# Output stage by d_ff chunks, PSUM banks by estimated end of use, attention tiles read behind a unit's sum: a cosformer attention and SwiGLU kernel

## The chip, the cores and the metric

One core of one Trainium2 chip. The metric is the device time of a run, in microseconds (us): the kernel before has a median of 316.65 us over 5 runs, from 316.18 to 317.08. TensorE (PE) multiplies into PSUM, which has eight banks of 128 partitions x 512 fp32. VectorE (DVE), ScalarE (ACT) and GpSimd (POOL) do the rest, and SyncE (SP), ACT and POOL issue DMAs, each in its own program order.

## The reference

```python
def phi(x, c, s):                       # q and k of shape (8, 8, 576, 64)
    r = np.maximum(x, 0.0)
    return np.concatenate([r * c, r * s], axis=-1)   # c, s: cos and sin of pi/2 * pos/576
kv  = einsum('bhsf,bhsd->bhfd', phi(k), v);  z = phi(k).sum(axis=2)
num = einsum('bhsf,bhfd->bhsd', phi(q), kv)
den = einsum('bhsf,bhf->bhs', phi(q), z)[..., None] + 1e-6
x = (num / den).transpose(0, 2, 1, 3).reshape(4608, 512)
out = (silu(x @ w_gate) * (x @ w_val)) @ w_out       # d_model 512, d_ff 1536, output fp32
```

## The kernel before

**Rows.** The 4608 tokens go in nine rows (`tg` 0 to 8) of 512 tokens, four tiles of 128 tokens each. A row has a hidden stage of twelve slots and an output stage of four. While a row computes, the next rows are prepared: `plan` maps a slot number (16 per row) to functions, `at` enters them, and `slot` calls them when the row's code comes to that slot. So the program order on every engine is written out by hand (`manual_schedule`).

**Hidden stage, rows 0 to 6** (`ffn_fc`): for each of the twelve chunks of d_ff, four matmuls of 512 columns for the gate and four for the value (`ffn_mm`, L564), silu on ACT (L570), the product of both on DVE into `ht` (L575). Two PSUM banks per chunk.

**Hidden stage, rows 7 and 8** (`GATE`, `ffn_by_quarters`): the gate product is a seven-product (Strassen-like) form, in three units `u` of four chunks. A unit has products of 4 matmuls x 256 columns (L621) into banks `a`, `b`, `c`, `e`; between them stand the four value products `V` (L633). ACT copies `a` into `b` (L649) and `e` into `m7` (L653); DVE adds `c = m7 + b` (L659) and `m7 += b` (L668); ACT takes silu (L627), DVE multiplies into `ht` (`mul`, L638). The sums of x that the form needs are L605, those of the weights L597.

**Output stage, rows 2 to 8** (`out_by_quarters`): the same seven-product form over halves of the tokens, of d_ff and of d_model. Order of the products, of 12 matmuls x 256 columns each (`product`, L786): `a`, `e = S3 T3`, `b += S2 T2`, `a +=`, `b += S1 T1`, `c += .. T4`, `b += S4 ..`. In `product` the token half `i` is the outer loop and the d_ff chunk `kc` the inner one. `S1` to `S4` are sums of pieces of `ht` (`token_sum`, L760), made by DVE as the chunks come. ACT copies `a` into `b` (L808) and evicts `e`, `a`, `c` (L811, L799); DVE does L816 (b into c), L827 (b into C22, after S1 T1) and L801 (the last eviction of b). In the last row `b` has a bank for each token half, and L801 and its stores go by halves.

**Preparation.** Per batch `b` of 576 tokens: POOL waits for the turned q of the batch before (`load_behind`, a copy at L998) and loads q, k, v (L131); `phi_q` takes the relu of q on ACT (L266) and multiplies by the cos/sin table on DVE (L283), a quarter at a time; `qturn_dma` turns the result by two DMA transposes on SP (L306); `relu_k` (ACT, L266) and `vmul` (DVE, L287) prepare k and v; `kv_mm` (L333) makes kv, `kv_out2` (L356) copies it out. Per token tile: `a_tile2` multiplies (L448, 8 matmuls, two banks), `x_of` normalises on DVE (L458, L467, L471), `x_turn` turns x by a DMA transpose on SP (L548). Its readers are the next row's matmuls.

**Stores.** `store` (L711) issues two DMAs of 64 partitions x 512 fp32 per tile, on SP; so SP's queue holds, in program order, the transposes of q and x and the stores of each row. The last row's stores are split between SP and ACT (`store_two`, L718).

**Banks.** `take` picks PSUM banks when the program is built: the free ones that were taken or given back longest ago (`touch`, counter `now`). From row 7 on (`loose`) a single bank is picked so that pairs are kept whole where possible. `a_tile2` takes two banks without holding them.

Of the kernel before, what the change touches and what calls it, by code (L numbers as in the profile page):

```python
# [18 lines left out]
def kernel(  # L19
# [32 lines left out]
    GATE = (7, 8)  # L52

# [23 lines left out]
    loose = [False]  # L77

    def take(n, hold=None, fills=False, seeded=False):

        taken = {x for r in held.values() for x in r}
        if loose[0]:
            free = [b for b in range(8) if b not in taken]
            if n == 1:
                bs = [min((b for b in free if filled[b] or not seeded), key=lambda b: (
                    not any(x != b and x + 1 != b and x + 1 in free for x in free), used[b]))]
            else:
                b0 = min((b for b in free if b + 1 in free), key=lambda b: max(used[b:b + 2]))
                bs = [b0, b0 + 1]
            if hold is not None:  # L90
                held[hold] = bs
            for b in bs:
                filled[b] = fills or seeded
            touch(bs)
            return banks[:, bs[0]] if n == 1 else banks[:, bs[0]:bs[0] + 2]
        free = [b for b in range(0, 8, n) if not any(b <= x < b + n for x in taken)
                and (filled[b] or not seeded)]

        b0 = min(free, key=lambda b: (n == 1 and hold is not None and hold[0] == "o" and b ^ 1 not in taken,
                                      sorted(used[b:b + n], reverse=True)))  # L100
        if hold is not None:
            held[hold] = range(b0, b0 + n)
        filled[b0:b0 + n] = [fills or seeded] * n
        touch(range(b0, b0 + n))
        return banks[:, b0] if n == 1 else banks[:, b0:b0 + n]

    def touch(r):
        now[0] += 1
        for x in r:
            used[x] = now[0]  # L110

    def give_back(hold):
        touch(held.pop(hold))
# [171 lines left out]

    def vmul(b, g):
        nc.vector.tensor_tensor(  # L287
            out=v2s[b == 1][:, g, :, :, 0:D],
            in0=(first if b == 0 and g == 0 else {"v": raw_of(b, "v")})["v"][:, g].unsqueeze(2).to_broadcast([P, NC, 2, D]),
            in1=tab, op=ALU.mult,  # L290
        )
# [56 lines left out]

    kv2s = [consts.tile([P, 2, J, 2, D1], BF16, name=f"kv2_{j}") for j in range(2)]

    def kv_out2(b):

        ps = st[b, "kvps"][:, :, 0:4 * J * D1 // 2].rearrange("p e (j w x) -> p e j w x", j=J, w=2)
        for w, eng in enumerate((nc.scalar.copy, nc.vector.tensor_copy)):
            for i in range(2):
                eng(out=kv2s[b % 2][w * D:(w + 1) * D, :, :, i], in_=ps[i * D:(i + 1) * D, :, :, w])  # L356

    def kv_free(b):
        give_back(("kv", b))
# [77 lines left out]
    def a_tile2(t):  # L437

        (b0, c0), (b1, c1) = (divmod(2 * t + r, NC) for r in range(2))
        ps = take(2)  # L440
# [12 lines left out]
        x_of(t, ps)  # L453
# [153 lines left out]
    def ffn_by_quarters(tg, slot_of):  # L607
# [7 lines left out]
        def free(nm):  # L615
            give_back(("g", tg, nm))

        def product(to, u, a, x, first):
            for i in range(2):
                for c in range(KH):  # L620
                    nc.tensor.matmul(out=to[:, i], lhsT=a[:, c, 2 * u + i], rhs=x[:, :, c],  # L621
                                     start=first and i == 0 and c == 0, stop=c == KH - 1, skip_group_check=True)
# [6 lines left out]
        def V(u, i, w):  # L629
            fc = 4 * u + 2 * i + w  # L630
            val[u, i, w] = take(1, ("v", tg, fc), fills=True)
            for kc in range(KC):
# [3 lines left out]
        def mul(u, i, w):  # L636
            fc = 4 * u + 2 * i + w
            nc.vector.tensor_tensor(out=ht[:, fc], in0=gates[u, w][:, i], in1=val.pop((u, i, w)), op=ALU.mult)  # L638
            give_back(("v", tg, fc))
# [5 lines left out]
        for u in range(3):  # L645
# [8 lines left out]
            free("e")  # L654
# [4 lines left out]
            nc.vector.tensor_tensor(out=c, in0=m7, in1=b, op=ALU.add)  # L659
            product(a, u, A12, B21, False)  # L660
            silu(u, 1, 0, a)
            free("a")
            if u:
                mul(u - 1, 1, 1)
# [3 lines left out]
            nc.vector.tensor_tensor(out=m7, in0=m7, in1=b, op=ALU.add)  # L668
            silu(u, 0, 1, m7)
            product(c, u, A22, X4, False)  # L670
            silu(u, 0, 0, c)
            free("c")
            V(u, 1, 0) if u else V(u, 0, 1)
            done()
            if u == 2:
                for n in (1, 2):
                    token_sum(n, 0, 4)
# [6 lines left out]
            free("b")  # L684
            if u:
                V(u, 0, 1)
            mul(u, 0, 1)
            if u:
                done()
                token_sum(*((3, 0, 4) if u == 1 else (4, 0, 4)))  # L690
# [31 lines left out]
    def ffn_out(t, f0=0, f1=None):  # L722
# [16 lines left out]
        store(t)  # L739
# [27 lines left out]
    def out_by_quarters(tg, slot_of):  # L767

        last = tg == NTG - 1
        t0 = tg * OUT  # L770
# [12 lines left out]
        def product(to, a, b, first):  # L783
            for i in range(2):
                for kc in range(HC):
# [31 lines left out]
        token_sum(4, 4, 6)  # L817
# [17 lines left out]
        else:  # L835
            for t in (t0 + 2, t0 + 3):
                store(t)
# [4 lines left out]
        for t in (t0, t0 + 1):  # L842
            store(t, *((slice(HD, d_model), (nc.sync, nc.scalar)) if last else ()))
# [152 lines left out]
    def load_behind(b):  # L996

        nc.gpsimd.tensor_copy(out=hold2, in_=phit[b - 1][0:1, :, 0, 0, 0])  # L998
        load(b, "q")
        if b > 3:  # L1000
            load_kv(b)

# [10 lines left out]
    for n in range(4):  # L1013
        at(SLOTS * (1 + n * (GATE[0] - 1) // 4) + FC + 3, lambda n=n: gate_weight_sum(n))
# [3 lines left out]
    for b in range(2, B):  # L1018
        s0 = SLOTS * (b - 1)
        keng = "dve" if b == 2 else "act"  # L1020
        steps = [lambda b=b, g=g: phi_q(b, g) for g in range(G)]
        steps += [lambda b=b, g=g: (relu_k(b, g, g + 1, keng), vmul(b, g)) for g in range(G)]
        if b == 2:
            fs, tq = [s0 + i for i in (0, 0, 1, 1, 4, 5, 5, 6)], (s0 + 2, s0 + 2)
        else:
            p0 = s0 - SLOTS
            fs, tq = [p0 + 12, p0 + 12] + [p0 + 11 + i for i in range(2, 8)], (p0 + 15, p0 + 16)
            if b == 3:
                fs, tq = [p0 + 12 + i for i in range(4)] + [s0 + 4, s0 + 4, s0 + 5, s0 + 5], (s0 + 2, s0 + 2)
            at(p0 + 3 if b < 5 else p0 + 1, lambda b=b: load_behind(b))  # L1030
        tk = (s0 + 4, s0 + {2: 8, 3: 7}.get(b, 5))
        for s, f in zip(fs, steps):
            at(s, f)
        for e in range(2):
            at(tq[e], lambda b=b, e=e: qturn_dma(b, e))
        at(tk[-1], lambda b=b: kv_mm(b), lambda b=b: kv_out2(b))
        at(tk[-1] + 1, lambda b=b: kv_free(b))
    for t in range(2 * OUT, NTG * OUT):
        tg, i = divmod(t, OUT)
        s = SLOTS * (tg - 1) + (5 if tg > 2 else 4) + 2 * i  # L1040
        if t == 2 * OUT:
            at(s, a_(t, 0))
            at(s + 1, a_(t, 1), turn(t))
        elif tg == 2:
            at((9, 10, 11)[i - 1] + SLOTS, lambda t=t: a_tile2(t), turn(t))
            if i == 2:
                at(11 + SLOTS, load_3)
        else:
            if t in (13, 14, 15):
                s = SLOTS * 2 + t - 4  # L1050
            elif tg - 1 in GATE:
                s = SLOTS * (tg - 1) + ((1, 2, 7, 9) if tg < 6 else (1, 2, 4, 7) if tg < 8 else (1, 2, 5, 6))[i]
            at(s, lambda t=t: a_tile2(t), turn(t))
    for tg in range(1, NTG):
        s0 = SLOTS * tg
        if tg in GATE:
            loose[0] = True
# [9 lines left out]
        for i in range(OUT):  # L1067
            ffn_out(tg * OUT + i)
# [33 lines left out]
```

## Time and profile before

| what | value |
|---|---|
| median of 5 runs | 316.65 us (316.18 to 317.08) |
| the profiled execution: its own time | 316.65 us |
| the profiled execution: span of the trace | 314.9 us |
| busy in the span: PE, DVE, ACT, POOL | 97%, 73%, 46%, 11% |
| granted TensorE clock | 1.00 |
| read from HBM, written | 37.75 MB, 9.44 MB |
| row 3 / 4 / 5 / 6 / 7 / 8 starts at (us of the span) | 120.3 / 152.7 / 185.7 / 218.1 / 250.5 / 281.4 |
| last matmul starts | 310.1 |

The span is counted from the first instruction to the last; 1.75 us of the execution's time lie outside it. The share of busy time is an average; the row starts are the first matmul of each row in the timeline of PE. A matmul record is longer than the distance to the next one, since matmuls are pipelined; so lost time is read from the distances between the starts of groups of matmuls, not from durations.

### The profile page before, as it was taken

To read this page: it belongs to the slowest core of one execution; us is meant where nothing else is said; L and a number is where in the kernel's file an instruction comes from. 1 tells how busy PE (TensorE), PEld (TensorE's weight loads), DVE (VectorE), ACT (ScalarE), POOL (GpSimd) and SP (SyncE) were. 2 spreads that over 40 slices of the span, in tenths; PEclk is the share of its full clock that TensorE was granted. 3 is DMA by queue.
4 is the path that set the end of the run, shared out by engine and by line. 5 is a ranking of instruction groups with operands and counts; after the bars stand their busy time and mean duration, and the time that the engine had idled before them with its cause. 6 is when DMAs were issued, how large, how long until landed. Compare 5 with 4: busy or idle time off the path is not lost.

```text
span 314.9 us, 6775 instructions
## 1 busy us (share of the span) xinstructions
PE 306.5 (97%) x2696; PEld 189.5 (60%) x2696; DVE 228.4 (73%) x458; ACT 143.7 (46%) x264; POOL 35.7 (11%) x62
## 2 busy tenths in 40 slices
PE   8899999999999999999999999999999999999994
PEld 3597455445444585548654764567456866687673
DVE  7874777697678888587748786787779478945772
ACT  8454555763335346334543454336533344324530
POOL 7854102000200200030003000300000000000000
PEclk9999999999999999999999999999999999999999
DMA  7999999996797995999495979598951160014004
GB/s 259 223 198 197 206 205 137 226 135 104 136 209 114 148 147 121 146 118 190 96 152 71 199 152 153 72 192 130 163 90 35 37 149 17 20 35 100 0 2 133
DMA packets 74767, 41.07 MB, mean 130 GB/s; under 512 B 49904, under 2 KB 69872, under 8 KB 74736
## 3 DMA queue, kind: packets, MB, share of 16 engines
q1 hardware_dynamic: 51952, 22.55, 39.1%
q0 software_dynamic: 22192, 17.57, 37.2%
q10 hardware_dynamic: 592, 0.52, 0.5%
q8 instruction: 21, 0.34, 0.5%
q14 instruction: 10, 0.08, 0.1%
HBM read 37.75 MB, written 9.44 MB: 150 GB/s over the span
## 4 chain that ended last, share of the span: by engine, by line
PE 87%; DVE 7%; DMA 2%; ACT 2%; issue 1%; DVEq 0%; ACTq 0%
PE banks L564 45%; PE banks L786 17%; PE banks L729 6%; PE banks L633 5%; PE banks L621 5%; PE banks L333 3%; PE banks L448 2%; DMA xT<-x 2%; DVE ht L638 1%; DVE sums L760 1%; DVE x L471 1%; PE banks L494 1%; PE banks L430 1%; DVE v L287 1%; DVE ht L575 1%
## 5 line engine op out<-in xcount | busy, mean ns | idle before, releaser
L564 PE MATMUL banks<-xT,wg_sb 128*128 128x512 f16 (+2 forms) x368 | 86.6, 360 | 0.2 <-DMA xT<-x 0.2
L564 PE MATMUL banks<-xT,wv_sb 128*128 128x512 f16 (+2 forms) x368 | 86.6, 360 | 0.0
L570 ACT ACTIVATE sg<-banks 128x512 bf16<-128x512 f32 (+2 forms) x92 | 51.5, 560 | 76.3 <-PE banks L564 73.7
L575 DVE TENSOR_TENSOR ht<-sg,banks 128x512 f16<-128x512 bf16 (+2 forms) x92 | 58.0, 637 | 29.9 <-PE banks L564 22.8
L564 PEld LDWEIGHTS <-wv_sb 128*128 128x128 f16 x368 | 35.5, 98 | 37.4
L564 PEld LDWEIGHTS <-wg_sb 128*128 128x128 f16 x368 | 33.9, 98 | 31.8 <-issue 0.5
L786 PEld LDWEIGHTS <-ht 128*128 128x128 f16 x336 | 32.5, 98 | 4.2
L786 PEld LDWEIGHTS <-sums 128*128 128x128 f16 x252 | 24.4, 98 | 4.2 <-issue 0.8
L633 PE MATMUL banks<-xT,wv_sb 128*128 128x512 f16 x96 | 24.3, 379 | 0.0
L283 DVE TENSOR_TENSOR r_q<-raw_q,tab 128x1152 bf16<-128x1152 bf16 x24 | 17.6, 754 | 7.4 <-ACT raw_q L266 7.1
L729 PE MATMUL banks<-wo_sb,ht 128*128 128x512 f16 x96 | 22.7, 379 | 0.0
L471 DVE TENSOR_TENSOR x<-banks,rec 128x512 f16<-128x512 f32 (+1 forms) x32 | 21.6, 674 | 1.3 <-PE banks L430 0.3
L786 PE MATMUL banks<-wo_sb,ht 128*128 128x256 f16 x168 | 20.6, 273 | 0.0
L287 DVE TENSOR_TENSOR v<-raw_v,tab 128x1152 bf16<-128x1152 bf16 x27 | 19.9, 751 | 0.3 <-ACT raw_v L849 0.3
L786 PE MATMUL banks<-wt_sb,sums 128*128 128x256 f16 x168 | 19.8, 273 | 0.1
L786 PE MATMUL banks<-wt_sb,ht 128*128 128x256 f16 x168 | 19.5, 272 | 0.0
L799 ACT ACTIVATE ob<-banks 128x512 f32<-128x512 f32 x14 | 8.4, 597 | 21.8 <-PE banks L786 21.8
L638 DVE TENSOR_TENSOR ht<-sg,banks 128x512 f16<-128x512 bf16 x24 | 15.5, 681 | 2.4 <-ACT sg L627 2.4
L266 ACT ACTIVATE raw_k<-raw_k 128x576 bf16<-128x576 bf16 (+1 forms) x25 | 17.0, 694 | 0.0
L760 DVE TENSOR_TENSOR sums<-ht 128x1024 f16<-128x1024 f16 (+1 forms) x28 | 15.5, 553 | 0.4
L998 POOL COPY hold<-phit 1x2 bf16<-1x2 bf16 x5 | 0.9, 177 | 128.5 <-DMA phit<-r_q 128.5
L266 ACT ACTIVATE raw_q<-raw_q 128x576 bf16<-128x576 bf16 x24 | 15.4, 675 | 0.0
(121 smaller groups left out, 333.8 us busy)
## 6 DMA issues: line engine op xcount, KB each, us to landing
out_dram<-ob SPq DMA_DIRECT2D x67, 128.0 KB, 2.4
raw_k<-in_k_dram POOLq DMA_DIRECT2D x7, 576.0 KB, 9.1
raw_q<-in_q_dram POOLq DMA_DIRECT2D x6, 576.0 KB, 6.5
raw_v<-in_v_dram POOLq DMA_DIRECT2D x6, 576.0 KB, 11.7
wo_sb<-in_moe_w_out_dram POOLq DMA_DIRECT2D x3, 512.0 KB, 12.8
wg_sb<-in_moe_w_gate_dram POOLq DMA_DIRECT2D x5, 256.0 KB, 9.1
wv_sb<-in_moe_w_val_dram POOLq DMA_DIRECT2D x5, 256.0 KB, 9.5
wo_sb<-in_v_dram SPq DMA_DIRECT2D x2, 576.0 KB, 4.3
```

The source lines that it names most:

```text
L266: nc.scalar.activation(out=out, in_=in_, func=AF.Relu)
L283: nc.vector.tensor_tensor(out=st[b, "q"][:, g], in0=o.unsqueeze(2).to_broadcast([P, NC, 2, D]), in1=tab, op=ALU.mult)
L287: nc.vector.tensor_tensor(out=v2s[b == 1][:, g, :, :, 0:D], in0=(first if b == 0 and g == 0 else {"v": raw_of(b, "v")})["v"][:, g].unsquee ...
L471: nc.vector.tensor_tensor(out=st["x", t].rearrange("p (y e d) -> p e y d", e=2, d=D)[:, :, ys], in0=ps[:, :, 0:2 * J * D1].rearrange("p e ...
L564: nc.tensor.matmul(out=st["f", tg, fc, lo][i], lhsT=(wg_sb, wv_sb)[i][:, kc, fs], rhs=xT[tg][:, ts, kc], start=(kc == 0), stop=(kc == KC - 1))
L570: nc.scalar.activation(out=sg[:, 0:n], in_=st["f", tg, fc, lo][0], func=AF.Silu, scale=DOWN)
L575: nc.vector.tensor_tensor(out=ht[:, fc, r:r + n], in0=st.pop(("s", tg, fc, lo))[:, 0:n], in1=ps[1], op=ALU.mult)
L633: nc.tensor.matmul(out=val[u, i, w], lhsT=wv_sb[:, kc, fc * P:(fc + 1) * P], rhs=xT[tg][:, :, kc], start=(kc == 0), stop=(kc == KC - 1))
L638: nc.vector.tensor_tensor(out=ht[:, fc], in0=gates[u, w][:, i], in1=val.pop((u, i, w)), op=ALU.mult)
L729: nc.tensor.matmul(out=o_ps[t], lhsT=ht[:, fc, r:r + P], rhs=wo_sb[:, fc], start=(fc == 0), stop=(fc == FC - 1))
L760: nc.vector.tensor_tensor(out=o[:, lo:hi], in0=x[:, lo:hi], in1=y[:, lo:hi], op=op)
L786: nc.tensor.matmul(out=to[i][:, 0] if len(to) == 2 else to[0][:, i], lhsT=a[:, kc, i * P:(i + 1) * P], rhs=b[:, kc], start=first and kc == ...
```

## The change

- `product` of the output stage has `kc` outermost and the token half `i` innermost.
- Stores of rows 1 to 7 are issued by POOL instead of SP.
- `take` in rows 7 and 8 picks the single free bank whose estimated end of use is earliest. The estimate is in matmul rows (`rows`, moved on by `LATE["M"]`, `["V"]`, `["O"]`, `["X"]`); `give_back` gets a lateness per use. `a_tile2` holds its banks until its x is recorded.
- In rows 7 and 8 an attention tile at certain slots puts its x (L458, L467, L471, L548) and the freeing of its banks into `behind`, which is emptied after `c = m7 + b` and after `m7 += b`. In the same way DVE's half of `kv_out2`. `mul(u - 1, 1, 1)` moves behind `m7 += b`; `S2` of the first chunks moves behind two more `mul`, `S4` of the first chunks into the output stage.
- Slots come from tables: `ROW` per batch (phi of q, turning, k and v, kv), `TILES` per row. Batch 3 and 4 stay; for batches 5 and 6 the phi of q moves from slots 12, 12, 13, 14 to 8, 9, 12, 12 and 6, 8, 9, 12, the turning from 15 and 16 to 13, k and v from 15 to 18 to 13 to 16. Tiles of rows 5 to 7 move from slots 5, 7, 9, 11 to 2, 4, 7, 9; those made in row 7 from 1, 2, 5, 6 to 0, 3, 5, 7.
- Batch 7's phi of q is 18 ACT instructions of 128 x 256 (`phi_q_part`) instead of 4 relus on ACT and 4 multiplies on DVE.
- q of batches 6 and 7 is loaded one row earlier, behind k and v of the batch before.
- The weight sums L597 are at the ends of rows 1, 2, 3, 4 instead of 1, 2, 4, 5.

The order of instructions is the same up to row 2 on PE, DVE and ACT, and the number of matmuls is the same (2696).

```diff
+    AHEAD = 6
+    WSUM = (31, 47, 63, 79)
+    ROW = {2: ((16, 16, 17, 17), 18, (20, 21, 21, 22), 8), 3: ((12, 13, 14, 15), 18, (20, 20, 21, 21), 7),
+           4: ((12, 12, 13, 14), 15, (15, 16, 17, 18), 5), 5: ((8, 9, 12, 12), 13, (13, 14, 15, 16), 5),
+           6: ((6, 8, 9, 12), 13, (13, 14, 15, 16), 5), 7: ([4 + i // 2 for i in range(18)], 13, (12, 13, 14, 15), 3)}
+    TILES = {2: (0, 9, 10, 11), 3: (5, 9, 10, 11), 4: (5, 7, 9, 11), 5: (2, 4, 7, 9), 6: (2, 4, 7, 9), 7: (2, 4, 7, 9), 8: (0, 3, 5, 7)}
+    LATE = dict(M=44, V=87, O=131, X=26, x=150, v=(190, 250, 120, 150), e=130, a=90, c=170, b=110, k=120)
...
-                bs = [min((b for b in free if filled[b] or not seeded), key=lambda b: (
-                    not any(x != b and x + 1 != b and x + 1 in free for x in free), used[b]))]
+                bs = [min((b for b in free if filled[b] or not seeded), key=lambda b: used[b])]
...
-    def touch(r):
+    def touch(r, late=1):
         now[0] += 1
+        if loose[0]:
+            for x in r:
+                used[x] = rows[0] + late
+            return
...
+    def phi_q_part(b, c, w):
+        if (b, "q") not in st:
+            st[b, "q"] = rel.tile([P, G, NC, 2, D], BF16, name="r_q")
+        nc.scalar.activation(out=st[b, "q"][:, :, c, w], in_=raws[b, "q"][:, :, c], func=AF.Relu,
+                             scale=csk[:, c, w:w + 1])
...
-        x_of(t, ps)
+        if later:
+            behind.append(lambda: (x_of(t, ps), give_back(("a2", t), LATE["x"]), x_turn(t)))
+        else:
+            x_of(t, ps)
+            give_back(("a2", t), LATE["x"])
...
             nc.vector.tensor_tensor(out=c, in0=m7, in1=b, op=ALU.add)
+            while behind:
+                behind.pop(0)()
             product(a, u, A12, B21, False)
             silu(u, 1, 0, a)
-            free("a")
-            if u:
-                mul(u - 1, 1, 1)
+            free("a", LATE["a"])
             V(u, 0, 0) if u else V(u, 1, 0)
             done()
             product(b, u, W1, X1, False)
             nc.vector.tensor_tensor(out=m7, in0=m7, in1=b, op=ALU.add)
+            while behind:
+                behind.pop(0)()
             silu(u, 0, 1, m7)
+            if u:
+                mul(u - 1, 1, 1)
...
             if u == 2:
-                for n in (1, 2):
-                    token_sum(n, 0, 4)
+                token_sum(1, 0, 4)
...
             mul(u, 0, 1)
+            if u == 2:
+                token_sum(2, 0, 4)
             if u:
                 done()
-                token_sum(*((3, 0, 4) if u == 1 else (4, 0, 4)))
+            if u == 1:
+                token_sum(3, 0, 4)
...
+        queues = (nc.gpsimd, nc.gpsimd) if tg > 0 else None
...
-            for i in range(2):
-                for kc in range(HC):
+            rows[0] += LATE["O"]
+            for kc in range(HC):
+                for i in range(2):
                     nc.tensor.matmul(out=to[i][:, 0] if len(to) == 2 else to[0][:, i],
...
-        token_sum(4, 4, 6)
+        token_sum(4, 0 if tg in GATE else 4, 6)
...
-                store(t)
+                store(t, queues=queues)
...
-        load(b, "q")
+        if b < AHEAD:
+            load(b, "q")
         if b > 3:
             load_kv(b)
+        if AHEAD <= b + 1 < B:
+            load(b + 1, "q")
```

## The prediction

> **What bounds the kernel now.** First the page's line of busy time.
>
> ```profile
> PE 306.5 (97%) x2696; PEld 189.5 (60%) x2696; DVE 228.4 (73%) x458; ACT 143.7 (46%) x264; POOL 35.7 (11%) x62
> ```
>
> PE has work nearly all the time. Then the busy time by row (stretch, length, PE, PEld, DVE, ACT, POOL, granted clock, DMA share, GB/s); rows 4, 6, 7 and 8:
>
> ```profile
> 152.60:185.70 33.10, 32.83 (x295) 19.59 (x294) 24.63 (x46) 15.34 (x27) 2.41 (x4) 1.00 0.83 138
> 218.20:250.50 32.30, 32.30 (x293) 19.55 (x291) 23.17 (x45) 12.31 (x22) 0.00 (x0) 1.00 0.48 86
> 250.50:281.40 30.90, 30.40 (x251) 22.11 (x249) 22.95 (x45) 12.27 (x22) 0.00 (x0) 1.00 0.24 52
> 281.40:310.40 29.00, 28.97 (x218) 20.93 (x215) 19.17 (x34) 12.19 (x23) 0.00 (x0) 1.00 0.22 52
> ```
>
> The clock is full; DVE has 7 to 10 us to spare in each row, ACT 17 or more. The matmuls stay the same 2696, so only PE's waits, its start and its tail can change. Busy PE hides short waits; I read them from distances between starts in PE's timeline (start, length, line). Without a wait, eight matmuls of 512 columns take 1.727 us (.216 each), twelve of 256 columns 1.30 (.1087 each).
>
> ```profile
> 182.03 1.91 PE L786 MATMUL banks<-wt_sb,ht 128*128 128x256 f16 x16
> 183.97 1.47 PE L786 MATMUL banks<-wo_sb,sums 128*128 128x256 f16 x12
> 185.68 1.02 PE L564 MATMUL banks<-xT,wg_sb 128*128 128x512 f16 x4 [0.24 <-DMA xT<-x]
> ...
> 256.67 0.60 PE L621 MATMUL banks<-xT,wg_sb 128*128 128x256 f16 x4
> 257.61 0.60 PE L621 MATMUL banks<-kvt,wgs_sb 128*128 128x256 f16 x4 [0.35 <-DVE x L471]
> ...
> 266.95 1.03 PE L633 MATMUL banks<-xT,wv_sb 128*128 128x512 f16 x4
> 268.05 0.60 PE L621 MATMUL banks<-kvt,wgs_sb 128*128 128x256 f16 x4
> ...
> 273.26 3.04 PE L786 MATMUL banks<-wt_sb,sums 128*128 128x256 f16 x24
> 276.13 1.04 PE L786 MATMUL banks<-wo_sb,ht 128*128 128x256 f16 x8
> ```
>
> From 182.03, sixteen matmuls need 1.74 and take 1.94: **.20** lost ahead of S4's product. From 183.97 to 185.68 is 1.71 for 1.30: **.41** before row 5, for xT. At 256.67 four need .435 and take .94: **.51** for L471's x, whose read frees the bank. From 266.95 it is 1.10 for .865: **.245**, c and m7 late behind an attention tile, sums and `mul`. From 273.26 it is 2.87 for 2.61: **.25**, for S2's last chunk (L760). In the same way: .20 before S4's product in rows 2, 3, 5 (.17 in row 3), .06 at 265.21, .13 in row 8 at 304.08. Behind 16 us these make 2.4 us in all; the losses before that lie ahead of the first reordered code.
>
> **The change part by part.** Sums are against this execution: its own time is 316.65 us, span 314.9 and 1.75 outside; that is also the median of the runs shown.
>
> *S4's product waits for the bank that L827 empties.* DVE's timeline in row 2 shows why that is late:
>
> ```profile
> 117.55 0.76 DVE L283 TENSOR_TENSOR r_q<-raw_q,tab 128x1152 bf16<-128x1152 bf16 x1
> 118.22 0.68 DVE L827 SCALAR_TENSOR_TENSOR ob<-banks,ob 128x512 f32<-128x512 f32 x1
> ```
>
> Multiplies of phi of q are ahead of L827, three to a row at .67 from start to start. Row 2 keeps them (batch 4's slots stay): nothing. Rows 3 and 4 lose them from the output stage, row 5 altogether: .17 + .20 + .20 = **.56** gained (rounded from .565). What is late next: L827 follows L816 at .65, and PE's 24 matmuls between (2.6) cover both.
>
> *xT before row 5.* The last tile's transpose was issued at 178.60 and landed at 185.54, while loads for batch 6 (issued 170.5 to 172) ran until 185.16. Now q of batch 6 is loaded a row earlier, and row 5's tiles are made at slots 2, 4, 7, 9 instead of to 11, some 3.5 us earlier (a slot is 1.73): **.41** gained.
>
> *Row 7's gates.* The e product gets another bank (the earliest free by the estimate), tiles come at slots 2, 4, 7, 9 behind c and m7, so c is no longer behind a tile's 1.05 us of DVE; S2's first chunks come later, two `mul` earlier. I put DVE's new order against PE's starts: e's bank is read .5 before it is wanted, c and m7 come .15 to .5 early. What the change puts behind them, x and its transpose on SP, is wanted a row later; its banks by PE's next tile, over three slots on. .51 + .06 + .245 = **.82**.
>
> *Chunks outermost in `product`.* S2's last sum was .25 late in row 7 and .13 in row 8. The last two chunks' first use moves from 4 matmuls (.43) into a product to 8 (.87): .44 more, over both. **.25 + .13 = .38** gained. Chunk order costs PE nothing that I see: the same weights and shapes.
>
> Gains: .56 + .41 + .82 + .38 = **2.17**.
>
> *The tail pays.* In the last row the two halves of b end apart now:
>
> ```profile
> 309.75 0.42 DVE L801 TENSOR_SCALAR ob<-banks 128x256 f32<-128x256 f32 x1 [1.54 <-PE banks L786]
> 310.39 1.50 ACTq L711 DMA_DIRECT2D out_dram<-ob  x2
> 310.41 0.42 DVE L801 TENSOR_SCALAR ob<-banks 128x256 f32<-128x256 f32 x1 [0.23 <-PE banks L786]
> ```
>
> Half 0 is complete six matmuls (.65) before half 1; with halves innermost, one (.11). Its L801 and store start .55 later; half 1's L801 stands behind it, .3 later. The first of ACT's two stores takes .75 of its 1.50, so the end moves by .1 to .55. I take **.5**, since ACT's pair is the last issue to end.
>
> *Stores to POOL.* In rows 1 to 7, 56 issues of .75 (L131's row on POOL) leave SP for POOL, whose 11% leave room. SP had eight of them in its way:
>
> ```profile
> 119.59 5.68 SPq L711 DMA_DIRECT2D out_dram<-ob  x8
> 125.37 7.70 SPq L306 DMA_TRANSPOSE phit<-r_q  x2
> ...
> 135.79 0.18 POOL L998 COPY hold<-phit 1x2 bf16<-1x2 bf16 x1 [30.55 <-DMA phit<-r_q]
> 136.24 0.75 POOL L131 DMA_DIRECT2D raw_q<-in_q_dram  x1 [0.28 <-PE banks L448]
> ```
>
> The transposes can start when r_q ends (120.92). From 125.37 to the second landing, 135.64, it took 10.27: so 121.0 + 10.27 = 131.3. A store waits on POOL for its eviction now, and behind it stand only the copy and the loads. POOL ends its eight stores at 119.7 + 8 x .75 = 125.7, so they are hidden; POOL's copy and loads go 4.4 earlier. Before, q of batch 5 landed at 142.62; in after it lands at about 138.3. It is now wanted at slot 8 of row 3, by its relu at about 137.9, and PE stands still only from 139.3 on. So it costs nothing, with 1.0 us to spare. The extra load (q of batch 6) adds 3.5 to 4 to the three loads' 13.6; the last tile's xT of row 3 then lands by 151.5, wanted at 152.6: nothing.
>
> POOL stores have a rule against them. "SBUF — State Buffer" of the Trainium skill, section "SBUF: two separate sides", says that issuing a DMA from GpSimd is held up while DVE runs an operation in a mode that takes both ports. At 170.5 to 172.7 POOL's three issues took .75, .75, .76 beside DVE's L575 and L760, and those took .68 to .69 as elsewhere: no hold-up is seen here. By the rule at its worst each store would wait for one DVE operation, 8 x (.75 + .69) = 11.5, ending at 131.2 instead of 125.7, still not behind the transposes' landing: no change of the sum by either.
>
> *Batch 7's phi of q on ACT* (18 pieces, table as scale). Row 5's DVE loses 4 x .75 = 3.0; ACT gets 18 operations instead of four at .675 (L266). None of this form stands in the trace. The nearest rows are L504, with a scale from a table on 128x260, at .476, and L266 itself, 576 wide, at .69; below L356's .375 nothing suggests. At .48 ACT has .56 (silu) + 2 x .48 = 1.52 in a slot of 1.73: hidden. At .69 it has 1.94, .21 too much in each of nine slots (less in the last, 8 count): 1.7 late, against .7 that the second pair of banks gives; **1.0** lost. I take .48, the like form; so nothing.
>
> *The weight sums* (3 x .95 in a row) move from the end of row 5 to that of row 3, behind its L801: DVE has 8 us to spare there: nothing; up to .2 if L575 of the next row's first slot comes late.
>
> Sum: 316.65 - 2.17 + .5 = **315.0 us**, span about 313.2. Own range 314.2 (tail .1, and .4 that short distances hid from me) to 315.8 (tail .55, a third of the gains given back).
>
> **Rivals.**
>
> - *ACT becomes the bound in row 5.* For it: two extra operations beside each silu; against: L504's .476. Price 1.0 from above: 316.0.
> - *It doesn't do what it says.* The planner's estimates put a bank or a tile no better than before: row 7 loses .8 elsewhere, rows 4 and 5 (.6) get other waits for xT. Left: 2.17 - 1.4 - .1 (S4 in one row) - .5 = .2: 316.5. For it: c and m7 have only .15 of slack. Against: the order by hand shows no such wait.
> - *Slower: q of batch 5 comes late in row 3.* Phi of q at slot 8 needs it at 137.9; before it landed at 142.62. If the transposes don't move up (SP held by something else, or the stores' packets delay them), it lands at 142.6, ACT's relu stands there with silu behind it, and both pairs of banks fill: PE loses 142.6 - 139.3 = 3.3. 316.65 + 3.3 - 1.65 = 318.3. It decides from a landing at 141.0 on (1.65 eaten). For it: four loads now share the queues, and stores come beside them; against: the 4.4 us by which the copy on POOL moves up.
>
> **How the numbers follow.** The forecast has .58, ACT as the bound .16, not as it says .10, late q .16. About 0.2% (.63 us) is what a measurement of this kernel can tell from no change. Faster: .58 and half of ACT's case, which ends at that edge: .66. Same: the other half and the third case: .18. Slower: .16. The range reaches from 314.2 over the first three cases to 317.0, since about .2 may be left out.
>
> **What the profile after would show.** Right: 2696 matmuls; S4's product late by .2 in row 2 alone; row 5 without idle time for xT; no distance over .1 too long in rows 7 and 8; the transposes of row 3 on SP at 121, POOL's copy at 131.5, q landing near 138; pieces of phi at .48; the end .5 further behind the last matmul. Wrong: L564 or L621 waiting for ACT in row 5 (long pieces), PE still at 139 to 143 (q), or tiles whose x, now behind a sum, hold the banks that the next product wants. Early losses ahead of 16 us should stand as they are.

## The result, and the profile after

The changed kernel takes a median of 318.91 us over 27 runs (316.47 to 323.66), the kernel before 316.72 over 47 (316.17 to 318.00); the ratio is 1.0048, with a 95% interval of 1.0037 to 1.0060. So it is slower by half a per cent, and the prediction (315.0, range 314.2 to 317.0) is wrong. The ratio leaves out executions far above the others; the first profile is of one of these, 322.26 us with a span of 320.5, and a second one, of an execution at 318.80, comes from experiment 13.

The line of busy time of the changed kernel:

```profile
PE 308.3 (96%) x2696; PEld 190.5 (59%) x2696; DVE 225.6 (70%) x452; ACT 148.0 (46%) x278; POOL 65.6 (20%) x118
```

The matmuls are the same 2696. The last starts at 315.62, 5.5 us later than before. By stretch (same columns as in the prediction; the stretches are those of the kernel before), two of them have idle PE, rows 3 and 5:

```profile
120.00:152.60 32.60, 30.18 (x265) 17.66 (x264) 24.20 (x46) 14.70 (x28) 7.43 (x13) 1.00 0.96 158
...
185.70:218.20 32.50, 29.99 (x248) 16.42 (x246) 20.55 (x39) 16.93 (x35) 5.94 (x11) 0.95 0.83 123
```

Row 5 has a clock of .95 as well. All waits that the prediction wanted gone are gone: row 7 goes through without a distance over .1 too long, row 5 doesn't wait for xT, S2's last chunk is in time in rows 7 and 8, S4's product is .2 late in row 2 alone. Where .51 was lost in row 7, the two starts are .43 apart now, as long as four matmuls take:

```profile
257.30 0.60 PE L651 MATMUL banks<-xT,wg_sb 128*128 128x256 f16 x4
257.73 0.60 PE L651 MATMUL banks<-kvt,wgs_sb 128*128 128x256 f16 x4
```

The loss is new. Row 3, in the timelines of PE, ACT, SP and POOL:

```profile
143.56 0.29 PE L473 MATMUL banks<-kv,phit 128*128 128x65 bf16 x4
144.25 0.29 PE L473 MATMUL banks<-kv,phit 128*128 128x65 bf16 x4 [0.40 <-DVE ht L604]
146.56 1.47 PE L825 MATMUL banks<-wo_sb,ht 128*128 128x256 f16 x12 [2.02 <-DVE x L500]
```

```profile
142.12 0.68 ACT L277 ACTIVATE raw_q<-raw_q 128x576 bf16<-128x576 bf16 x1 [4.00 <-DMA raw_q<-in_q_dram]
142.71 0.58 ACT L599 ACTIVATE sg<-banks 128x512 bf16<-128x512 f32 x1
```

```profile
121.60 11.01 SPq L323 DMA_TRANSPOSE phit<-r_q  x2
```

```profile
120.38 4.21 POOL L748 DMA_DIRECT2D out_dram<-ob  x8 [14.13 <-ACT ob L838]
134.38 0.18 POOL L1037 COPY hold<-phit 1x2 bf16<-1x2 bf16 x1 [9.79 <-DMA phit<-r_q]
134.87 0.79 POOL L142 DMA_DIRECT2D raw_q<-in_q_dram  x1 [0.31 <-issue]
```

Read it from the bottom up. POOL's stores go out at 120.4 to 124.6, as forecast; the transposes start at 121.60, as forecast. But now they run beside each other: the two transposes' issue takes 11.01 on SP (7.70 before), the second lands at 134.23 instead of 131.3, POOL's load follows at 134.87, and q of batch 5 lands at 142.10, 7.2 behind its issue (6.4 before). ACT's relu (L277) of slot 8 stands 4.00 us for it, with silu (L599) behind; PE fills its banks and loses .56 + 2.19 = 2.75 us.

Row 5, in the timelines of PE, ACT and SP:

```profile
205.37 0.29 PE L473 MATMUL banks<-kv,phit 128*128 128x65 bf16 x4 [1.43 <-DVE ht L604]
206.74 0.37 PE L473 MATMUL banks<-kv,phit 128*128 128x65 bf16 x4 [1.08 <-ACT sg L599]
206.92 1.90 PE L593 MATMUL banks<-xT,wg_sb 128*128 128x512 f16 x4
208.61 1.81 PE L593 MATMUL banks<-xT,wv_sb 128*128 128x512 f16 x4
```

```profile
196.46 0.60 ACT L599 ACTIVATE sg<-banks 128x512 bf16<-128x512 f32 x1 [1.14 <-PE banks L593]
203.22 0.91 ACT L300 ACTIVATE r_q<-raw_q,cs_all 128x256 bf16<-128x256 bf16 x2 [6.16 <-DMA xT<-x]
```

```profile
185.04 10.64 SPq L323 DMA_TRANSPOSE phit<-r_q  x2
```

ACT's first piece of batch 7's phi (L300) stands 6.16 us. The profile puts xT as the releaser, but this piece reads only q and the table. What ended at 203.07 is the second transpose of batch 6, and it reads `r_q`, which has a single buffer: the piece writes the buffer that the transpose still reads. That transpose took 14.42 us from its issue, beside eight stores, and the pair 18.0 from the first issue. PE loses 1.60 + 1.24 us, and then L593 goes at half speed for eight matmuls (1.90 for four): 1.6 more.

Sum: 310.10 (last matmul before) - 2.17 (the gains, as forecast) + 2.75 + 2.84 + 1.6 + .5 (the first 119 us, in which the matmuls started later in this execution) = 315.6. It closes, so only these two places need a cause.

### The profile page after: what moved, and what is told of

Read it like the earlier page. It is cut to its first block, busy times and chain, and to the rows that moved or that the text cites. A ratio compares the mean times of both kernels' runs of the same rounds, so it can differ in the third digit from the quotient of the medians.

```text
span 320.5 us, 6798 instructions
## 1 busy us (share of the span) xinstructions
PE 308.3 (96%) x2696; PEld 190.5 (59%) x2696; DVE 225.6 (70%) x452; ACT 148.0 (46%) x278; POOL 65.6 (20%) x118
## 4 chain that ended last, share of the span: by engine, by line
PE 82%; DMA 10%; SPq 2%; DVE 2%; ACT 2%; issue 1%; DVEq 0%; POOL 0%; POOLq 0%; ACTq 0%
PE banks L593 38%; PE banks L825 20%; PE banks L766 7%; PE banks L664 6%; PE banks L651 6%; DMA phit<-r_q 3%; DMA ht<-in_k_dram 3%; DMA xT<-x 2%; DMA raw_q<-in_q_dram 2%; PE banks L473 2%; PE banks L350 2%; SPq L323 1%; PE banks L523 1%; SPq L171 1%; PE banks L454 1%
## 5 line engine op out<-in xcount | busy, mean ns | idle before, releaser
L593 PE MATMUL banks<-xT,wg_sb 128*128 128x512 f16 (+2 forms) x368 | 87.6, 363 | 0.0
L593 PE MATMUL banks<-xT,wv_sb 128*128 128x512 f16 (+2 forms) x368 | 87.4, 363 | 0.1
L599 ACT ACTIVATE sg<-banks 128x512 bf16<-128x512 f32 (+2 forms) x92 | 51.3, 559 | 69.8 <-PE banks L593 63.6
L593 PEld LDWEIGHTS <-wv_sb 128*128 128x128 f16 x368 | 35.7, 99 | 38.1 <-issue 1.4
L748 POOL DMA_DIRECT2D out_dram<-ob x56 | 29.4, 534 | 125.8 <-ACT ob L838 121.0
L593 PEld LDWEIGHTS <-wg_sb 128*128 128x128 f16 x368 | 33.7, 98 | 31.0 <-issue 1.0
L294 DVE TENSOR_TENSOR r_q<-raw_q,tab 128x1152 bf16<-128x1152 bf16 x20 | 14.7, 753 | 6.3 <-ACT raw_q L277 6.2
L277 ACT ACTIVATE raw_k<-raw_k 128x576 bf16<-128x576 bf16 (+1 forms) x25 | 16.7, 694 | 0.0
L473 PEld LDWEIGHTS <-phit 128*128 128x128 bf16 (+1 forms) x240 | 10.4, 101 | 10.2 <-issue 4.6
```

The source lines that it names most:

```text
L277: nc.scalar.activation(out=out, in_=in_, func=AF.Relu)
L473: nc.tensor.matmul(out=ps[ms, e, g * D1:(g + 1) * D1], lhsT=phit[b][:, e, g, c:c + n].rearrange("p c s -> p (c s)"), rhs=kv2s[b % 2][:, e, ...
L593: nc.tensor.matmul(out=st["f", tg, fc, lo][i], lhsT=(wg_sb, wv_sb)[i][:, kc, fs], rhs=xT[tg][:, ts, kc], start=(kc == 0), stop=(kc == KC - 1))
L599: nc.scalar.activation(out=sg[:, 0:n], in_=st["f", tg, fc, lo][0], func=AF.Silu, scale=DOWN)
L748: (queues or (nc.sync, nc.sync))[e].dma_start(out=out_v[idx // NC, idx % NC][:, cols], in_=ob_of(t)[e * SH:(e + 1) * SH, cols])
```

## The experiments

Theory 1: slots were moved ahead of what they need; phi of batch 5 stands for q's landing, batch 7's for the buffer `r_q`. Theory 2: stores on POOL now run beside the transposes of q and lengthen them, so that things land later than the prediction had them. Rival 3: the planner's banks, the tiles behind sums, or a full ACT cost time.

**1: batch 5's old slots.**

```diff
-           5: ((8, 9, 12, 12), 13, (13, 14, 15, 16), 5),
+           5: ((12, 12, 13, 14), 15, (15, 16, 17, 18), 5),
```

> The changed kernel, with batch 5's phi of q, turning and k and v put back to the slots they had before (12, 12, 13, 14; 15; 15 to 18); all else as changed. Theory 1 (slots that want data too early): in row 3 the relu of slot 8 stood for q of batch 5, which landed at 142.10, and PE lost 0.56 + 2.19 = 2.75 us between 143.6 and 146.6. With the old slots that wait is gone: 2.7 us less than the changed kernel, no gap above 0.3 us in row 3; the stall of row 5 (2.84 us and a clock of half for 8 matmuls after it) stays. S4's product is .2 late in row 3 again. Theory 2 (stores on POOL run beside the transposes of q, which then take 12.6 to 18.0 us from first issue to last landing instead of 10.3 to 11.9): it gains the same 2.7 here, since the late landing hurts only the early slots; but it says that transposes keep their 12.6 and more. Rival 3 (the planner's banks or the tiles behind sums hold PE): row 3 keeps its gap, no change.

314.90 median (314.69 to 320.21, 12 runs), ratio to the kernel before .9947 (.9930 to .9964): 4.0 below the changed kernel, more than the 2.7 expected, and faster than before. No gap in rows 3 and 5, S4's product .2 late in rows 2 and 3. The last matmul starts at 308.02, 2.08 ahead of the kernel before: the prediction's gains less row 3's .17 are 2.0. q landed at 141.51, as late as ever; nobody stood for it. In row 5 the first piece still stood 3.13 us (transposes 15.1 from first issue to POOL's copy behind them), but PE's banks covered it:

```profile
197.08 0.91 ACT L300 ACTIVATE r_q<-raw_q,cs_all 128x256 bf16<-128x256 bf16 x2 [3.13 <-DMA xT<-x]
```

**2: phi of batch 7 in its own buffer.**

```diff
...
-            st[b, "q"] = rel.tile([P, G, NC, 2, D], BF16, name="r_q")
+            st[b, "q"] = raw_q[:, 1:3].rearrange("p n g c d -> p (n g c d)").rearrange("p (g c w d) -> p g c w d", c=NC, w=2, d=D)
```

(in `phi_q_part`; `raw_q`, a pool of three buffers before, is made one tile of three, of which batch 7 uses the first)

> The changed kernel, with phi of q of batch 7 written to two raw_q buffers that are idle by then instead of the single r_q buffer; same slots, same 18 pieces on ACT. Theory 1: the first piece, at slot 4 of row 5, stood 6.2 us for the transposes of batch 6 that still read r_q (landed 203.07), silu behind it; PE lost 1.60 + 1.24 us, then 1.6 by the halved clock. Without the shared buffer these are gone: 2.8 to 4.4 us less than a run that has them, nothing in row 5 above 0.2; the 2.75 of row 3 stay. The pieces take .45 to .48 each. Theory 2 gives the same here. Rival 3 (ACT is too full in row 5 with 18 pieces of .46, about two per slot): row 5 loses 1.0 or more even without the shared buffer.

318.96 median (317.37 to 321.08, 7 runs), ratio 1.0071 (1.0043 to 1.0099). In the profile, at 317.37, the piece goes without a wait and row 5 is whole, so the buffer was the wait; ACT's pieces take .45 each and don't fill ACT, so that part of rival 3 falls. Row 3 still loses .12 + 2.19 = 2.3. But the other runs are no faster than the changed kernel, so row 5 isn't what makes its usual time.

```profile
196.10 0.89 ACT L300 ACTIVATE raw_q<-raw_q,cs_all 128x256 bf16<-128x256 bf16 x2
```

**3: all stores on SP.**

```diff
-        queues = (nc.gpsimd, nc.gpsimd) if tg > 0 else None
+        queues = None
...
-            ffn_out(tg * OUT + i, queues=(nc.gpsimd, nc.gpsimd))
+            ffn_out(tg * OUT + i)
```

> The changed kernel with all stores on SP again, in the order of the program; the slots as changed. Theory 1 alone (the slots are too early whatever the queues do): row 3 stalls 3.3 (q of batch 5 lands at 142.6 as before), row 5 still stalls about 2.8; time as the changed kernel, within 1 us. Theory 2 (the stores beside the transposes make these late): the transposes of batch 6 are issued ahead of row 4's stores and land 10.3 to 11.9 after their first issue, at 9 us into row 5 instead of 15; row 5 loses under 0.5 and keeps its clock: 3 to 4 us less than a run of the changed kernel that has the stall. Row 3 still loses 3.3, because there the transposes stand behind the eight stores on SP.

322.40 median (320.31 to 324.22, 6 runs), ratio 1.0171 (1.0136 to 1.0207). Theory 2 is right in row 5: the transposes of batch 6, ahead of the stores on SP now, took 9.9 us instead of 18.0, and PE lost nothing there. In row 3 both theories were right in kind and I was short in size: the transposes started at 126.59 behind the stores, q landed at 145.71, and PE lost 6.3 us, then 1.6 by a halved clock. With PE still from 139.3 on, the prediction's price formula gives 145.7 - 139.3 = 6.4.

```profile
145.74 0.68 ACT L277 ACTIVATE raw_q<-raw_q 128x576 bf16<-128x576 bf16 x1 [7.61 <-DMA raw_q<-in_q_dram]
```

**4: 1 and 2 together.**

> Both: batch 5's old slots, and batch 7's phi of q in its own buffer; stores on POOL, banks, tiles, output order as changed. Theories 1 and 2: no stall in rows 3 and 5, clock 1.00; what the prediction counted as gains is left, less the .17 of row 3: 315.2 us, 1.5 below the kernel before, and all runs within 1 us of each other. Rival 3: something else of the change costs as well, 316.5 or more.

315.72 median (315.00 to 320.06, 12 runs), ratio .9968 (.9953 to .9982). The profile, at 315.32, has no stall; but the median is .8 above experiment 1. Between the two profiles, .2 is a later start and .4 lies behind the last matmul (5.3 us to the end of the span; 4.9 in experiment 1). Experiment 2 ends 5.3 behind it too, but so do experiments 3 (5.4) and 7 (5.3), which don't have the tile of three buffers; so the tile isn't shown to be the cause, and the longer end stays open.

**5: slots as changed, q of batch 5 loaded a row earlier.**

```diff
-    AHEAD = 6
+    AHEAD = 5
```

> The changed kernel with its early slots, but q of batch 5 too is loaded a row earlier (AHEAD 5 instead of 6): in row 2, behind q, k and v of batch 4. Theory 1 (the early slots of row 3 stand for q's landing, and for nothing else): the relu at slot 8 finds its q, the gap of 2.2 to 2.8 us in row 3 is gone. In its place a fourth load stands in row 2: it ends about 3.5 later, at 120.6, and with it xT of row 3's last tile, wanted at 120.3: up to 1 us lost there. 316 to 317, with single runs higher where row 5 stalls. Rival (the work of slot 8 and 9 itself is too much for ACT and DVE in row 3): the gap stays though q is there.

315.72 median (315.06 to 316.92, 12 runs), ratio .9968 (.9953 to .9983). The relu of slot 8 runs at once, at 137.66, and row 3 has no gap: it was the landing of q, not the work. xT of the last tile landed at 119.72, in time for row 3. In this profile (316.62) row 5 loses 1.9 behind `r_q`.

```profile
137.17 0.60 ACT L599 ACTIVATE sg<-banks 128x512 bf16<-128x512 f32 x1 [1.39 <-PE banks L593]
137.66 0.68 ACT L277 ACTIVATE raw_q<-raw_q 128x576 bf16<-128x576 bf16 x1
```

**6: the kernel before, with batch 5's early slots alone.**

```diff
+            if b == 5:
+                fs, tq = [p0 + i for i in (8, 9, 12, 12, 13, 14, 15, 16)], (p0 + 13, p0 + 13)
```

> The kernel before with one part of the change: phi of q of batch 5 at slots 8, 9, 12, 12 of row 3, its turning at 13, k and v at 13 to 16. Theory 1: q lands at 142.6 as in the kernel before, PE stands still from 139.3 on, so 3.3 us lost, .2 gained at S4 in row 3 (it is no longer behind multiplies): 319.8; 321.4 where the clock halves after the stall. Rival (the stall needs the stores on POOL): no stall, 316.5.

321.72 median (321.33 to 322.52, 5 runs), ratio 1.0151 (1.0131 to 1.0172), as theory 1 has it for a halved clock. q landed at 142.76; PE lost .78 + .78 + 2.19 = 3.75, and then 25 distances of matmuls were doubled. So this one part makes the loss, without any store on POOL:

```profile
144.01 0.29 PE L448 MATMUL banks<-kv,phit 128*128 128x65 bf16 x4 [0.61 <-ACT sg L570]
144.91 0.29 PE L448 MATMUL banks<-kv,phit 128*128 128x65 bf16 x4 [0.61 <-DVE ht L575]
147.22 1.01 PE L786 MATMUL banks<-wo_sb,ht 128*128 128x256 f16 x4 [2.02 <-DVE x L471]
```

**7: experiment 1 with all stores on SP** (the edits of 1 and 3).

> Experiment 1 (batch 5's old slots) with all stores on SP again. Theory 2 (stores on POOL lengthen the transposes, SP's stores delay their start, and PE waits for neither now): transposes take 10 to 11 us from first issue to landing in row 5 instead of 12 to 15, they start 4 later in row 3; time the same as experiment 1 within .4 (314.7 to 315.3), with fewer single runs above 317. Rival (stores on POOL bring part of the gain): 315.5 or more, with a wait for xT or q in rows 3 to 5.

317.15 median (316.46 to 319.54, 12 runs), ratio 1.0016 (.9997 to 1.0035): 2.25 above experiment 1, so the rival holds. The transposes started at 126.01, four loads followed from 138.88 to a last landing at 155.76, and row 4 stood for its last tile's xT:

```profile
155.08 1.04 PE L593 MATMUL banks<-xT,wg_sb 128*128 128x512 f16 x4 [2.22 <-DMA xT<-x]
```

In row 5 the transposes took 9.9 as in experiment 3. So stores on POOL lengthen the transposes, and yet pay: without them the transposes of row 3 land at 138.28 instead of 134.06 (experiment 1), the four loads end 3.9 later (155.76, 151.86 in experiment 1), and xT is late. Here, and in experiment 3, the pair took 12.3 in row 3, where the kernel before had 10.27 in the same order on SP; why isn't known.

**8: the kernel before, chunks outermost in `product`.**

```diff
-            for i in range(2):
-                for kc in range(HC):
+            for kc in range(HC):
+                for i in range(2):
```

> The kernel before with chunks outermost in the output product, nothing else. By the prediction's steps: the waits of .25 (row 7) and .13 (row 8) for S2's last chunk go, and the end lies .1 to .5 further behind the last matmul: 316.4 to 316.8, no change that can be told. Rival (the order of the products changes something else, such as weight loads that PE waits for): a steady excess in L786's starts, 0.5 us or more over seven rows.

316.42 median (316.06 to 316.82, 12 runs), ratio .9982 (.9972 to .9992). S2's waits in rows 7 and 8 are gone, the other waits stand (that for xT before row 5 is .16 in this profile); the end is 4.9 us behind the last matmul's start instead of 4.8.

**9: experiment 1 with the old choice of single banks.**

```diff
-                bs = [min((b for b in free if filled[b] or not seeded), key=lambda b: used[b])]
+                bs = [min((b for b in free if filled[b] or not seeded), key=lambda b: (
+                    not any(x != b and x + 1 != b and x + 1 in free for x in free), used[b]))]
...
-        if loose[0]:
-            for x in r:
-                used[x] = rows[0] + late
-            return
```

> Experiment 1 (no stall in row 3) with the choice of single banks as in the kernel before: pairs kept whole, order of use by the counter. The prediction's step for row 7: without the estimate, products of row 7 get banks that an attention tile still holds; the e product waits .3 to .6, c's or b's products some tenths: .5 to .9 us more than experiment 1 (315.4 to 315.8). Rival (the new slots and order on DVE alone take these waits away): the same as experiment 1, and nothing over .1 in row 7.

315.06 median (314.79 to 315.86, 5 runs), ratio .9946 (.9926 to .9966): as experiment 1, nothing over .1 in rows 7 and 8. The rival holds: the estimate of the banks' end of use brings nothing that shows. (Row 4 waited .3 for xT in this profile, where the fourth load landed at 152.2; so did experiment 14, .2.)

**10: experiment 1 with the tiles' x at once, not behind a sum.**

```diff
-            later = tg - 1 in GATE and s in (0, 1, 3, 4, 7, 8)
+            later = False
```

> Experiment 1, with the attention tiles of rows 7 and 8 normalised on DVE at once instead of behind c = m7 + b and m7 += b. The prediction's step: c stands behind 1.05 us of a tile's DVE work again; a product of row 7 waits .2 to .3 at two or three places: .3 to .8 more than experiment 1 (315.2 to 315.7). Rival (the tiles' new slots are enough): the same as experiment 1, no gap above .1.

316.35 median (315.69 to 317.92, 12 runs), ratio .9985 (.9967 to 1.0002): 1.4 above experiment 1. Row 7 loses .32, .25, .14 and .26, two of these here (L690 is c = m7 + b); .27 in row 5 is the `r_q` wait.

```profile
253.08 1.03 PE L664 MATMUL banks<-xT,wv_sb 128*128 128x512 f16 x4
254.26 0.60 PE L651 MATMUL banks<-kvt,wgs_sb 128*128 128x256 f16 x4 [0.16 <-DVE banks L690]
...
266.71 1.03 PE L664 MATMUL banks<-xT,wv_sb 128*128 128x512 f16 x4
267.82 0.60 PE L651 MATMUL banks<-kvt,wgs_sb 128*128 128x256 f16 x4
```

**11: the kernel before, stores of rows 1 to 7 on POOL.**

```diff
+        if 4 <= t < 32:
+            queues = (nc.gpsimd, nc.gpsimd)
```

> The kernel before, with the stores of rows 1 to 7 issued by POOL, nothing else. The prediction: costs nothing; transposes of rows 2 to 5 start 4 to 5 us earlier and land 4.4 earlier, q of batch 5 at 138.3. Theory 2: the stores run beside the transposes, which take 12.6 or more instead of 10.3; they start 4.3 earlier and land 1.5 to 2 earlier, q of batch 5 at 141.5; row 5's wait for xT (.41) goes, since the loads end earlier: 316.2 to 316.8.

316.25 median (316.02 to 316.96, 11 runs), ratio .9982 (.9971 to .9993). The transposes went from 121.14 to 134.05, 12.9 us; q landed at 141.80. Row 5's wait for xT is gone, the others stand (S2's in row 7 with .13 instead of .25).

```profile
121.14 11.05 SPq L306 DMA_TRANSPOSE phit<-r_q  x2
134.20 0.18 POOL L1000 COPY hold<-phit 1x2 bf16<-1x2 bf16 x1 [10.10 <-DMA phit<-r_q]
```

**12: experiment 5, batch 7's pieces from slot 6, last row's products with token halves outermost.**

```diff
-7: ([4 + i // 2 for i in range(18)], 13, (12, 13, 14, 15), 3)}
+7: ([6 + i * 7 // 18 for i in range(18)], 13, (12, 13, 14, 15), 3)}
...
-            for kc in range(HC):
-                for i in range(2):
+            for kc, i in [(k, j) for j in range(2) for k in range(HC)] if last else [(k, j) for k in range(HC) for j in range(2)]:
```

> Both causes mended: experiment 5 (q of batch 5 loaded a row earlier, early slots kept), batch 7's 18 pieces from slot 6 to 12 instead of 4 to 12 (3.5 us later, more than the 1.9 by which they stood in experiment 5), and the last row's products with the token halves outermost as in the kernel before (tail: .1 to .5 less). Theory 1: no stall in rows 3 and 5: 314.2 to 314.7, nearly all runs within .7 of each other. Rival (ACT is the bound in row 5 with 2.6 pieces of .46 and a silu of .56 per slot of 1.73): .5 to 1 lost in row 5, 315.0 to 315.6.

315.32 median (315.15 to 315.70, 5 runs), ratio .9948 (.9930 to .9966). No stall in rows 3 and 5, ACT isn't the bound; but the fourth load in row 2 ended at 120.07, and row 3 stood .71 for xT. The last matmul was at 308.60, the end 4.8 behind it, and S2's wait in row 8 is back (.13): halves in the last row bring nothing.

```profile
120.86 1.02 PE L593 MATMUL banks<-xT,wg_sb 128*128 128x512 f16 x4 [0.55 <-DMA xT<-x]
```

**13: the changed kernel again.**

> The changed kernel once more, for a profile of an execution at its usual 319 us (the first one shows 322.3, with a stall in row 5 that most executions need not have). Theory 1: the usual time is 315.0 plus row 3's stall of 2.2 to 2.9 plus 1.6 by a clock at half speed for some 3 us after it: a profile at 318.5 to 319.5 shows a clock of .994, steps of .43 instead of .216 (or .21 instead of .11) for 3 us behind row 3's stall, and nothing over .3 in row 5. Rival (the usual loss is row 5's): row 3 as in the first profile at full clock, 1 to 2 us lost in row 5.

317.91 median (316.77 to 323.10, 12 runs), ratio 1.0035 (1.0017 to 1.0052). Six runs lie at 316.8 to 317.5 with a clock of .999 or more, five at 318.4 to 319.3 with .993 to .996, one at 323.10 with .988. The profile, at 318.80, has row 3's stall, .72 + 2.19 = 2.91, nothing in row 5, and this behind the stall (stretches of the same columns):

```profile
144.00:147.00 3.00, 0.98 (x8) 0.69 (x8) 2.93 (x7) 0.53 (x2) 0.00 (x0) 0.75 1.22 202
147.00:150.00 3.00, 3.00 (x21) 2.31 (x19) 2.86 (x8) 0.57 (x1) 0.00 (x0) 0.68 1.21 206
150.00:153.00 3.00, 3.00 (x29) 2.69 (x28) 1.53 (x4) 1.76 (x4) 0.00 (x0) 1.00 0.47 91
```

```profile
146.24 2.72 PE L825 MATMUL banks<-wo_sb,ht 128*128 128x256 f16 x12 [2.02 <-DVE x L500]
```

Twelve matmuls of 256 columns started over 2.5 us instead of 1.3, and so the usual 319 is experiment 1's 314.9, less .2 (S4 in row 3), + 2.9 + 1.3 = 318.9; the rival falls.

**14: experiment 1 with batch 7's pieces from slot 6** (the first edit of 12).

> Experiment 1 (batch 5's old slots), and batch 7's 18 pieces from slot 6 on instead of 4. Theory 1 and 2: experiment 1's single runs at 317.4 and 320.2 are executions in which the transposes of batch 6, beside the stores, landed more than 3 us later than in its profile, so that the first piece stood; 3.5 us more room takes them away: 314.7 to 315.2, no run above 316. Rival (those runs have another cause): 1 or 2 of 10 still above 317.

314.92 median (314.70 to 315.30, 5 runs), ratio .9946 (.9934 to .9958), none above 315.3 where experiment 1 had two of twelve at 317.4 and 320.2. That fits theory 2, but five runs are few, and experiment 4 speaks against it: its piece doesn't wait for `r_q`, and it has two of twelve at 317.36 and 320.06 too. What makes these single runs stays open. Experiments 1, 9 and 14 have the lowest ratios, .9946 to .9947: some .5% below the kernel before.

## Why the prediction was wrong

- **The step that failed: "So it costs nothing, with 1.0 us to spare"**, of q of batch 5. It rested on "From 125.37 to the second landing, 135.64, it took 10.27: so 121.0 + 10.27 = 131.3". 10.27 was measured behind the stores; moved to 121, the transposes run beside them and took 12.6. Experiment 11, with nothing changed but the stores, has 12.9. The landing moved up by 1.4 instead of 4.4, q by .5 (142.62 to 142.10) instead of 4.3: 2.9 of the shortfall is the transposes, .9 comes behind them, most of it q's own load. Nor was 10.27 steady: in the trace before, the pairs of rows 4 to 6, behind stores too, took 11.9 to 12.0, and 1.7 more would have eaten the 1.0 to spare. The slots then need what isn't there: experiments 1, 5 and 6 show it from three sides. The prediction's rival of late q is what happened, at nearly its price: it named 139.3 as the start of the stall, and 142.1 - 139.3 = 2.8 is the 2.75 measured.
- **The halved clock was in no price.** About half of the executions lose 1.3 to 1.7 more behind the stall. So the rival's 318.3 lies between the two groups of experiment 13.
- **Batch 7's phi on ACT: "I take .48, the like form; so nothing".** The pieces took .45; the rival with ACT as the bound falls. What the step missed is what the piece writes: `r_q` has one buffer, and slot 4 comes before the transposes have read it. Of the moved step I had counted what it reads and issues, not what it overwrites. It cost 2.8 + 1.6 in the first profile, 1.9 in experiment 5's, nothing in experiment 13's.
- **The gains held.** S4: .2 stays in row 2 alone. xT before row 5: gone, and experiment 11 gets the same from stores on POOL alone, by loads that end 2.5 us earlier, a way that the step didn't name. `product`: .38 gone in experiment 8. Row 7: .82 gone, but not by all that the step named: the estimate that was to give the e product another bank isn't needed, since the old choice of banks loses nothing with the new slots (experiment 9). Tiles behind c and m7 are: without them row 7 loses .97 (experiment 10).
- **The tail was mis-sized:** .5 taken, .1 measured (span end behind the last matmul's start: 4.8 before, 4.9 in the changed kernel, experiments 1 and 8), the lower bound; but .5 to .6 in experiments 2, 3, 4 and 7, for a cause that stays open. The last issue ends .3 later (2.07 behind the last matmul's start, 1.79 before), but only 2.8 instead of 3.0 us pass from there to the end of the span in the changed kernel:

```profile
315.82 0.76 DVE L840 TENSOR_SCALAR ob<-banks 128x256 f32<-128x256 f32 x2 [1.86 <-PE banks L825]
316.27 1.13 SPq L748 DMA_DIRECT2D out_dram<-ob  x2
316.27 1.42 ACTq L748 DMA_DIRECT2D out_dram<-ob  x2
```

- **"The extra load", put at nothing,** held only while stores are on POOL. With them on SP row 4 waits 2.4 for xT (experiment 7; later transposes have a part in it, and the extra load alone wasn't tried), and even with them on POOL xT came .2 to .3 late in two profiles (9 and 14).

Without row 3's stall, and with row 5's hidden, the changed kernel takes 314.9 (experiment 1) where 315.0 was forecast. Some of this nearness is luck: experiment 1 gives up .2 of the gains (S4 in row 3), and the tail cost .4 less than was taken.

## What to carry to other kernels

A duration measured behind other work isn't the duration beside it: when a move takes a queue's work from in front of a transfer, price the transfer at what it takes with that work running too. Before moving a step ahead, list for each operand when it lands and for each output buffer who still reads it; a wait at the head of an in-order engine stops all behind it. Give a step that is moved up no less slack than the spread of its slowest transfer: here 5 us of it and more, from 12.3 to 18.0 beside stores.

## What the runs showed of the hardware

- **Stores beside transposes lengthen them.** A pair of q transposes takes 9.9 to 12.3 us from first issue to last landing with no stores from POOL beside it, 12.3 to 18.0 beside six to eight stores of 128 KB from POOL. In rows 3 to 5 SP's time for issuing the pair grows with it, from 7.5 to 9.1 up to 9.3 to 11.9:

```profile
184.40 7.54 SPq L323 DMA_TRANSPOSE phit<-r_q  x2
192.05 5.77 SPq L748 DMA_DIRECT2D out_dram<-ob  x8
```

(SP's timeline in experiment 7, transposes ahead of stores; 11.01 in row 3 of the changed kernel, shown above.)

- **PE's clock falls to half after a stall of under 3 us, by stretches of 3.41 us.** Behind row 5's stall the first profile grants half a clock from 206.78 to 210.19. The four half-speed times between 16 us and the last matmul in these runs last 3.41 (first profile, experiment 13) or 6.83 (experiments 3 and 6, of which 5.4 in experiment 6 lie behind its stall). Stretches laid back from 206.78 in steps of 3.41 show row 3's and row 5's stall in the same execution, and those of experiment 6 its stall (columns as in the prediction):

```profile
141.92:145.33 3.41, 2.22 (x17) 1.09 (x16) 2.49 (x4) 2.71 (x5) 0.00 (x0) 1.00 1.22 198
145.33:148.75 3.42, 2.19 (x21) 1.96 (x21) 3.32 (x9) 0.57 (x1) 0.00 (x0) 1.00 1.23 204
...
203.36:206.78 3.42, 0.91 (x9) 0.42 (x8) 1.60 (x4) 3.38 (x9) 1.59 (x3) 1.00 0.42 40
206.78:210.19 3.41, 3.41 (x12) 1.34 (x12) 2.75 (x6) 3.25 (x8) 0.00 (x0) 0.50 1.21 206
```

```profile
142.39:145.80 3.41, 1.58 (x13) 0.76 (x12) 2.30 (x4) 2.72 (x5) 0.00 (x0) 1.00 1.20 199
145.80:149.21 3.41, 1.99 (x10) 1.40 (x10) 3.34 (x8) 0.00 (x0) 0.00 (x0) 0.50 1.16 200
149.21:152.63 3.42, 3.42 (x18) 2.36 (x17) 1.90 (x6) 0.67 (x2) 0.00 (x0) 0.50 0.05 11
```

Row 3's stall of 2.75 us lay across two stretches with 2.2 us of PE work in each, and the clock stayed; row 5's of 2.84 lay in one with .91, and the clock halved. The other profiles fit, where stretches are laid back in the same way from a change of the clock (in experiments 2, 5 and 7 from the one behind the last matmul). At full speed the clock halved after .53, 1.54 and 1.58 us of work in a stretch (experiments 3, 13 and 6), and not after 1.81, 1.91 and 2.04 (7, 5 and 2). At half speed it came back after 2.70 and more (13), and not after .76 and 1.99 (3 and 6). So where a stall falls decides whether it costs nothing more or 1.3 to 2.6 us more. "TensorE: Matmul & The Clock Gate" of the Trainium skill, Part 1, says that a window of about 3.4 us, running freely, decides: one idle window halves the clock, one busy window restores it. The traces agree, and show that a window with 1.58 us of work in it still counts as idle, one with 1.81 doesn't.
- **A store issued on POOL takes .53** (4.21 for eight), less than the .75 by which the prediction bounded it from a load; no hold-up beside DVE's work is seen in this row.
